# First five chunks of a retention and spatial-gating kernel evicted in two steps with ready tables, and the steps of its head newly ordered

## Chip, cores and metric

The kernel runs on one core of a Trainium2 chip. The metric is the device time of one execution in microseconds; of several executions the median counts.

## What is computed

Inputs are q, k, v of shape (4, 8, 768, 64), float32. First a linear attention with a decay per head (retention), then an MLP with a spatial gate:

```python
state = gamma * state + outer(k[t], v[t])
y[t] = scale * (q[t] @ state)
x = y as (4, 768, 512)
h = relu(x @ w_in);  u, v = h[..., :512], h[..., 512:]
v_n = (v - mean(v)) / sqrt(var(v) + 1e-6)
v_s = w_spatial @ v_n + b_spatial
out = (u * v_s) @ w_out
```

## The kernel before

The work is cut into 24 chunks of 128 positions, six for each of four batches. Within a chunk two heads share the 128 partitions, so that a chunk is four head pairs. A chunk of retention has these steps. `scale_values` (letter p) multiplies v by the inverse decay; a first digit chooses the engine, and `p202` to `p206` are eight ScalarE instructions each. `ret_scores` (q) makes the products of keys and queries, `ret_mask` (j) masks them on VectorE. `total_sum` (t) adds the outer products of k and v to a running sum in PSUM, for half a chunk at a time, and with a first digit 1 it issues the next chunk's scores between. `total_copy` (k) copies this sum to SBUF, two ScalarE copies for each half. `out_products` (y) makes the chunk's output in two halves. `out_evict` (E) takes it out of PSUM, multiplied by the decay of its position. `out_half` splits it into a high part (h, rounded to float32r) and a low part (l). From chunk 5 on the sum is rebuilt per chunk (S and x).

The weights arrive as int64 words that hold doubles. Each of twelve pieces goes through a (ScalarE), c0 to c4 (VectorE), H (ScalarE: rounded high part), R and Q (VectorE or GpSimd: low part). Three float32r products (high times high, high times low, low times high) stand for one exact product.

`v_products` (V) are 12 matmuls for each chunk: four pieces k, three products each. After these come r (relu), s, A, e, w, n, N (normalization), u and z (the other half of w_in), P (spatial products), g, i, f, d (gate), o (output), Z (store).

The order of everything is written out by hand in the string `STEPS` (lines 24 to 85), one word per step. Each engine runs its own steps strictly in that order, through `keep`, and so does the SyncE queue that issues the loads (G, J: groups of q, k, v; L: weights; K: spatial weights; B: bias). So a step that waits holds back all that stands behind it on the same engine. U is a matmul on zeros into a PSUM tile that nobody reads; ten of them run before the first data arrive, and eight more stand between the steps of the first chunks.

What the change touches lies mostly before the word u7 of `STEPS`, some 96 us into the span: batch 0 and the weights. The multiplication at the eviction (lines 475 to 482) is one instruction for each head pair, with two factors:

```python
nc.vector.scalar_tensor_tensor(
    xf[:, hp], t[hp % 2][:, hp // 2].rearrange("p i c -> p (i c)"),
    qg_t[:, c, hp : hp + 1], qd_t[:, hp], ALU.mult, ALU.mult)
```

`qd_t` (the decay within a chunk) is a table that the kernel makes itself: VectorE spreads 8 columns over a diagonal (`decay_rows`, line 828), one float32 matmul spreads the rows over the partitions (`decay_spread`), ScalarE copies the result (`decay_copy`, line 835).

Of the kernel before, what the change touches and what calls it, by code (L numbers as in the profile page):

```python
# [9 lines left out]
F32 = mybir.dt.float32  # L10
# [80 lines left out]
THIRD = (5, 6)  # L91
SPLIT = ((0, 1), (2, 3), (4, 7), (12, 13), (5, 6), (10, 8), (9, 11))
# [3 lines left out]
def tile_retention_gmlp(  # L96
# [8 lines left out]
    decay: bass.AP,  # L105
    out: bass.AP,
# [24 lines left out]

    mask_t = wpool.tile([P, C], F32, name="mask_t")
    ND = 3 * NC * NP
    consts_t = wpool.tile([P, ND + NP * P // C], F32, name="decay_t")
# [4 lines left out]

    LINE = 64 // 4  # L140
# [99 lines left out]
    def split_high(i):  # L240
        keep(nc.scalar.copy(doubles[i][0], halves[i][1]))
# [35 lines left out]
    def spatial_high(n, s):  # L277
        keep(nc.scalar.copy(parts_sp[n][0][:, s], wholes[n][s]))

    def spatial_low(n, s):  # L280
        high, low = parts_sp[n]
        keep(residue(nc.vector, low[:, s], wholes[n][s], high[:, s]))
# [526 lines left out]
    for r in ROWS:  # L809
        nc.gpsimd.memset(pick_t[r, r], 1.0)  # L810
# [120 lines left out]
```

## Time and profile before

| | us |
|---|---|
| median of 3 runs | 369.53 |
| lowest, highest | 369.22, 370.04 |
| the profiled execution, its own time | 370.09 |
| its span, first to last instruction | 368.1 |
| TensorE busy | 360.3 |
| VectorE busy | 238.0 |
| ScalarE busy | 156.1 |
| GpSimd busy | 114.5 |

The span is what the trace shows; 2.0 us of the execution's own time lie around it. Matmuls overlap, and their modelled ends make TensorE look busier than it is, so that a stretch with little useful work can still read 80% busy. The distance between the starts of two matmuls tells more than their durations.

### The profile page before, as it was taken

The numbers are of one execution on the slowest core, as the hardware profiler recorded it, in microseconds if no ns is written. First come the engines' busy times: TensorE is split into PE (matmuls) and PEld (weight loads), VectorE is DVE, ScalarE is ACT, GpSimd is POOL, SyncE is SP. The second block draws the span as 40 slices with busy tenths as digits, with TensorE's granted clock in tenths as the row PEclk, the third lists the DMA queues.
The fourth block names the chain that finished last, engine by engine and source line by source line (L and its number), as shares of the span: only waits on it lengthen the run. The fifth ranks groups of instructions, "written<-read, shape, count | busy, mean of one in ns | idle before, by whom it ended". The sixth has DMA issues, their size and how long they took to land.

```text
span 368.1 us, 10328 instructions
## 1 busy us (share of the span) xinstructions
PE 360.3 (98%) x4428; PEld 314.0 (85%) x4428; DVE 238.0 (65%) x533; ACT 156.1 (42%) x322; POOL 114.5 (31%) x121
## 2 busy tenths in 40 slices
PE   7899999999999999999999999999999999999996
PEld 3677885879888889998988889999998888999985
DVE  2997999698875767698585562368685452165631
ACT  3797784443423355632313246342232235432232
POOL 3612531371053324241425341133133322404011
PEclk9999999999999999999999999999999999999999
DMA  7974786002253530303333214123303002000022
GB/s 303 397 265 190 294 312 268 0 12 105 88 174 116 173 120 28 116 3 116 116 115 119 84 59 144 36 80 116 118 0 122 24 2 87 0 0 2 1 87 85
DMA packets 13005, 41.20 MB, mean 112 GB/s; under 512 B 1440, under 2 KB 1696, under 8 KB 12960
## 3 DMA queue, kind: packets, MB, share of 16 engines
q1 hardware_dynamic: 12816, 40.42, 29.6%
q8 instruction: 35, 0.57, 0.7%
q10 hardware_dynamic: 144, 0.13, 0.1%
q14 instruction: 10, 0.08, 0.1%
HBM read 34.25 MB, written 6.29 MB: 110 GB/s over the span
## 4 chain that ended last, share of the span: by engine, by line
PE 93%; DMA 2%; ACT 1%; SPq 1%; DVE 1%; issue 0%; POOL 0%; POOLq 0%
PE u L161 18%; PE v L161 18%; PE o L161 18%; PE y L161 10%; PE sp L161 8%; PE x L161 6%; PE z L161 5%; PE s L161 3%; PE w L161 3%; PE d L161 2%; DMA vk<-in_float_dram 2%; PE total L161 1%; SPq L164 1%; ACT third L345 1%; ACT third L378 0%
## 5 line engine op out<-in xcount | busy, mean ns | idle before, releaser
L161 PE MATMUL u<-xh,winu_w 128*128 128x384 f32 x256 | 68.3, 338 | 0.0
L161 PE MATMUL v<-winv_w,xh 128*128 128x512 f32 x192 | 60.6, 397 | 0.0
L161 PE MATMUL o<-wout_w,gh 128*128 128x512 f32 (+1 forms) x192 | 59.3, 390 | 0.0
L475 DVE SCALAR_TENSOR_TENSOR xf<-x,decay_t,qd_t 128x128 f32<-128x128 f32 x96 | 29.2, 343 | 31.3 <-PE x L161 25.2
L161 PEld LDWEIGHTS u<-xh,winu_w 128*128 128x128 f32 x256 | 46.5, 188 | 0.7
L161 PE MATMUL u<-xl,winu_w 128*128 128x384 f32 x128 | 42.8, 335 | 0.0
L161 PE MATMUL y<-sp,a 128*128 128x384 f32 x216 | 41.8, 336 | 0.0
L161 PEld LDWEIGHTS v<-winv_w,xh 128*128 128x128 f32 x192 | 35.2, 188 | 7.4
L161 PEld LDWEIGHTS o<-wout_w,gh 128*128 128x128 f32 x192 | 35.2, 188 | 6.8
L573 POOL TENSOR_TENSOR vn<-vn 128x384 f32<-128x384 f32 x24 | 24.8, 1032 | 49.7 <-DVE a L167 40.5
L589 ACT CAST a<-vn 128x384 fp32r<-128x384 f32 x42 | 21.0, 512 | 42.8 <-POOL vn L573 26.7
L161 PE MATMUL v<-winv_w,xl 128*128 128x512 f32 x96 | 37.6, 392 | 0.8 <-issue 0.8
L161 PEld LDWEIGHTS y<-sp,a 128*128 128x128 f32 x216 | 37.6, 188 | 0.4
L161 PE MATMUL o<-wout_w,gl 128*128 128x512 f32 (+1 forms) x96 | 37.2, 388 | 0.0
L167 DVE TENSOR_TENSOR a<-vn,a 128x384 fp32r<-128x384 f32 x42 | 23.7, 577 | 13.5 <-ACT a L589 13.2
L650 ACT ACTIVATE ur<-u 128x384 f32<-128x384 f32 x32 | 15.2, 488 | 36.1 <-PE u L161 31.0
L539 POOL TENSOR_TENSOR rs<-rs,mhalf 128x1 f32<-128x1 f32 x24 | 15.0, 631 | 49.3 <-DVE rs L535 46.4
L352 POOL TENSOR_TENSOR vk<-vk,decay_t 128x512 f32<-128x512 f32 x17 | 19.1, 1123 | 35.9 <-DMA vk<-in_float_dram 35.9
L526 DVE BATCH_NORM_STATS2 bst<-vr 128x6 f32<-128x512 f32 x24 | 16.4, 687 | 18.9 <-ACT vr L519 18.9
L161 PE MATMUL s<-qk 64*64 64x64 f32 x768 | 27.8, 220 | 0.0
L161 PEld LDWEIGHTS s<-qk 64*64 64x64 f32 x768 | 25.0, 135 | 2.5 <-issue 2.2
L428 DVE TENSOR_TENSOR ws<-d,ws 64x256 f32<-64x256 f32 x54 | 22.8, 422 | 6.4 <-PE d L161 4.9
(120 smaller groups left out, 670.8 us busy)
## 6 DMA issues: line engine op xcount, KB each, us to landing
qk<-in_float_dram SPq DMA_DIRECT2D x24, 512.0 KB, 4.7
vk<-in_float_dram SPq DMA_DIRECT2D x20, 512.0 KB, 4.9
raw<-in_int_dram SPq DMA_DIRECT2D x12, 512.0 KB, 6.3
out_dram<-ot SPq DMA_DIRECT2D x23, 256.0 KB, 2.0
wst<-in_float_dram SPq DMA_DIRECT2D x4, 576.0 KB, 7.1
third<-in_float_dram SPq DMA_DIRECT2D x3, 512.0 KB, 9.2
values<-in_float_dram SPq DMA_DIRECT2D x1, 552.0 KB, 4.3
bsp_t<-in_float_dram SPq DMA_DIRECT2D x1, 384.0 KB, 6.0
```

Of the source, the lines that this page charges most:

```text
L161: keep(nc.tensor.matmul(out, lhs, rhs, start=start, stop=stop, skip_group_check=shared))
L164: keep(nc.sync.dma_start(dst, src))
L167: return eng.tensor_tensor(out, whole, high.bitcast(F32), ALU.subtract)
L345: keep(nc.scalar.mul(v, v, f))
L352: keep(engine.tensor_tensor(values[g], values[g], vd, ALU.mult))
L428: keep(nc.vector.tensor_tensor(dst[ROWS[r]], u, states[g][ROWS[r], i], ALU.add))
L475: nc.vector.scalar_tensor_tensor(xf[:, hp], t[hp % 2][:, hp // 2].rearrange("p i c -> p (i c)"), qg_t[:, c, hp : hp + 1], qd_t[:, hp], ALU ...
L526: keep(nc.vector.bn_stats(st, norm[b, c][0]))
L539: keep(nc.gpsimd.tensor_tensor(rs, rs, mhalf, ALU.pow))
L573: nc.gpsimd.tensor_tensor(*{7: (a11, a11, a21, ALU.subtract), 5: (a21, a21, a22, ALU.add), 6: (a21, a22, a11, ALU.subtract), 3: (a21, a12, ...
L589: keep(nc.scalar.copy(t[:, 0], part_whole(b, p, m)))
L650: keep(nc.scalar.activation(u, pu[:, :HALF], AF.Relu))
```

## The change

Four parts. (1) Chunks 0 to 4, and 6, 12 and 18 (the first ones of the other batches), are evicted by two `tensor_tensor` on two head pairs each, with one factor, instead of four `scalar_tensor_tensor`. (2) Each of the first five chunks has its own ready table. The host sends decay rows cut into three bf16 parts, 30 rows with a selection matrix beside them (69 KB), loaded by a DMA that ScalarE issues (m20). For each table one bf16 matmul spreads them over the partitions (m0 to m4, 30 rows by 512 columns) and ScalarE copies the result (m10 to m14). The diagonal product on VectorE and its GpSimd memsets and selects go. (3) Many steps may choose their engine by a digit: some relus, rounded copies and residues go from ScalarE to VectorE or from VectorE to GpSimd or back. V can be issued in two parts, two products that need only the high weights (V1...) and the one that needs the low weights (V2...). (4) The words of `STEPS` up to u7 are newly ordered; after that only four E words go.

```diff
-    "G0 v p0 U10 q0 j0 L0 L2 a0 m2 t00 m0 k000 k001 t01 y00 U301 y01 c00 c01 c02 c03 a2 c20 c21 "
-    "c22 G1 k011 k010 H0 m1 E00 L1 U201 U101 U501 q1 p1 t10 k100 k101 a1 t11 U401 U701 G2 k111 "
-    "E02 c23 E01 k110 E03 h0 j1 y10 c04 c24 c10 y11 E10 E13 E12 E11 c11 c12 p202 t20 k201 k200 L3 "
-    "a3 H1 h1 R0 Q0 l0 q2 V00 G3 G4 t21 k211 k210 c13 c30 c31 j2 l101 c14 q3 y20 y21 G5 E20 E23 "
-    "E22 E21 j3 c32 R101 Q1 p203 t130 k301 k300 U601 V10 U801 H2 h2 l102 t131 j4 k310 k311 p204 "
-    "y30 y31 E30 E31 R102 Q102 c33 c34 V20 t140 L5 k401 k400 H3 E32 a5 E33 h3 c50 c51 c52 l103 "
-    "c53 c54 V01 V21 V11 V22 V12 t141 k411 k410 R3 Q3 V02 V03 V23 y40 p205 t50 y41 E40 E41 E42 "
-    "E43 L4 r0 r2 k501 s0 A0 a4 h4 k500 c40 c41 j5 G6 G7 q6 V13 V30 V31 V32 V33 H5 R5 y50 y51 s2 "
...
+    "U10 G0 q0 U301 p100 m20 m0 m10 m1 L0 j0 a0 c00 t00 k000 y00 m3 m13 U201 c01 c02 c03 k001 y01 "
+    "t01 G1 E00 E02 k011 c04 q1 k010 m11 v p1 j1 h0 L2 a2 m2 c20 l100 c21 L1 a1 c10 U101 U501 "
+    "U401 L3 t10 k100 k101 t11 c22 c23 c24 a3 y10 y11 E10 G2 k111 H0 q2 m12 U701 U601 k110 R100 "
+    "p202 t20 c30 k201 k200 U801 E12 m4 j2 Q0 G3 p203 V1000 V2000 G4 t21 k211 y20 y21 q3 h101 "
+    "l101 c11 c12 c13 c14 L5 k210 t130 H1 V1010 V2010 V1011 V1001 G5 k301 E20 E22 k300 j3 h2 y30 "
+    "t131 y31 R01 H2 c31 l102 V1020 m14 Q101 V2001 V2011 V1012 p204 V1002 R102 Q02 V2020 V1021 "
+    "V2021 V2002 L4 c32 k311 G6 E30 V1022 j4 E32 V2022 a5 k310 t140 L6 c33 H3 V1003 c34 a4 c40 "
+    "V2012 h3 G7 k400 k401 c41 c42 R103 Q3 y40 c50 t141 k411 k410 y41 E40 p205 E42 V1023 V1013 j5 "
+    "V2013 c51 c52 V2003 r100 h4 V2023 s0 t50 k501 c53 k500 q6 l03 y50 y51 E50 E52 E53 V1030 a6 "
+    "A0 e0 r2 l4 s2 E51 H5 R5 c54 A2 e2 w2 h5 c43 c44 L8 l105 w0 n0 V2030 V1031 V2031 V1032 V1040 "
...
+    "V2052 K0 u1 V1053 z1 Q04 a8 W1 a9 L10 c60 c61 c62 c63 c90 c91 w3 H6 n3 N3 V2053 R06 r105 s5 "
+    "a7 c92 A5 w4 n4 N4 c93 u4 e5 z4 w5 n5 N5 S6 x600 G8 c80 c70 c71 c72 c64 u0 c73 Q106 c81 c82 "
+    "B P1 g1 i1 f1 P2 c74 P0 c83 H8 c84 R8 H7 z0 d01 H9 R109 c94 Q09 g0 u2 z2 g2 W2 Q108 a10 c100 "
...
         t, xf = evicted[g]
         outs[g] = xf
+        if c == 0 or g < TABLES:
+            for n in (s // 2 for s in steps if s % 2 == 0):
+                both = t[n].rearrange("p h i c -> p h (i c)")
+                keep(nc.vector.tensor_tensor(xf[:, n::2], both, tables[c][:, n::2], ALU.mult))
+            return
...
+        three = ((xh, high), (xh, low), (xl, high))
+        for x, w in (three, three[::2], three[1:2])[part]:
+            n = begun[b, c] = begun.get((b, c), 0) + 1
+            mm(norm[b, c], x[:, k, cols], w, start=n == 1, stop=n == 3 * KT)
...
-    def decay_copy():
-        keep(nc.scalar.copy(qd_t.rearrange("p h c -> p (h c)"), spread.pop(0)))
+    def decay_load():
+        keep(nc.scalar.dma_start(sown_t, rows))
+
+    def decay_spread(c):
+        spread[c] = ps_m.tile([P, NP * P], F32, tag="m", name=f"spread{c}")
+        mm(spread[c], pick_t[:, c * P : c * P + P], rows_t, True, True)
+
+    def decay_copy(c):
...
+        keep(nc.scalar.copy(tables[c].rearrange("p h c -> p (h c)"), spread.pop(c)))
```

## Rows read from the trace of the kernel before

**Rows 1.** The page: its span, busy time of TensorE, granted clock in 40 slices.
```profile
span 368.1 us, 10328 instructions
...
PE 360.3 (98%) x4428; PEld 314.0 (85%) x4428; DVE 238.0 (65%) x533; ACT 156.1 (42%) x322; POOL 114.5 (31%) x121
...
PEclk9999999999999999999999999999999999999999
```

**Rows 2.** Windows: us, busy of the engines (instructions), clock, DMA share, GB/s.
```profile
10.00:15.00 5.00, 4.08 (x104) 2.96 (x100) 4.92 (x12) 3.04 (x7) 2.74 (x2) 1.00 1.03 416
...
50.00:60.00 10.00, 10.00 (x40) 7.06 (x39) 9.83 (x23) 6.97 (x12) 3.15 (x4) 1.00 1.02 408
```

**Rows 3.** Waits of TensorE: us in total, times, longest.
```profile
PE total L161 <- ACT ws L378: 0.9, 1, 0.9
PE v L161 <- issue: 0.8, 1, 0.8
```

**Rows 4.** Chain that ended last, from 21 to 43 us: start, us, what.
```profile
21.33 1.16 PE x L161 x64
...
30.85 0.75 issue
...
40.96 1.09 PE x L161 x64
```

**Rows 5.** DMA issues, one short window each (issued 3.73, 4.22, 4.75, 5.76 us).
```profile
raw<-in_int_dram SPq DMA_DIRECT2D x1, 512.0 KB, 8.9
...
qk<-in_float_dram SPq DMA_DIRECT2D x1, 512.0 KB, 10.8
...
third<-in_float_dram SPq DMA_DIRECT2D x1, 512.0 KB, 11.5
...
raw<-in_int_dram SPq DMA_DIRECT2D x1, 512.0 KB, 11.8
```

**Rows 6.** Timeline of ScalarE: start, us, line, operation, names, idle before.
```profile
16.38 2.02 ACT L345 ACTIVATE third<-third,decay_t 128x64 f32<-128x64 f32 x8
18.43 0.75 ACT L378 COPY third<-total 64x256 f32<-64x256 f32 x2
...
21.46 2.02 ACT L345 ACTIVATE vk<-vk,decay_t 128x64 f32<-128x64 f32 x8
...
32.86 0.75 ACT L378 COPY third<-total 64x256 f32<-64x256 f32 x2 [2.06 <-PE total L161]
```

**Rows 7.** Groups by shape, ScalarE and VectorE, 5 to 45 us: busy, mean ns.
```profile
L207 ACT ACTIVATE room<-raw 128x512 f32<-128x512 f32 x6 | 4.0, 675 | 2.0 <-DMA raw<-in_int_dram 1.9
...
L241 ACT CAST winv_w<-df 128x512 fp32r<-128x512 f32 x4 | 2.5, 618 | 0.0
...
L835 ACT COPY qd_t<-spread 128x512 f32<-128x512 f32 x1 | 0.6, 586 | 0.0
...
L475 DVE SCALAR_TENSOR_TENSOR xf<-x,decay_t,qd_t 128x128 f32<-128x128 f32 x24 | 6.9, 341 | 2.0 <-PE x L161 1.9
```

**Rows 8.** The page, its groups of instructions and its DMA issues.
```profile
L428 DVE TENSOR_TENSOR ws<-d,ws 64x256 f32<-64x256 f32 x54 | 22.8, 422 | 6.4 <-PE d L161 4.9
...
out_dram<-ot SPq DMA_DIRECT2D x23, 256.0 KB, 2.0
```

**Rows 9.** Timelines of VectorE and GpSimd where the two meet.
```profile
15.39 1.49 DVE L212 TENSOR_SCALAR room<-room 128x512 f32<-128x512 f32 x1
...
16.81 1.12 DVE L475 SCALAR_TENSOR_TENSOR xf<-x,decay_t,qd_t 128x128 f32<-128x128 f32 x4
...
15.01 1.59 POOL L249 TENSOR_TENSOR winv_w<-df,room 128x512 fp32r<-128x512 f32 x1 [0.73 <-DVE room L238]
...
16.56 1.46 POOL L167 TENSOR_TENSOR xl<-xf,xh 128x512 fp32r<-128x512 f32 x1
```

**Rows 10.** Chain that ended last, where TensorE never waits: start, us, what.
```profile
113.90 1.09 PE x L161 x64
...
126.64 6.12 PE v L161 x27
```

More of the change, by code (lines that the diff above doesn't have):

```diff
@@ L91 @@
 THIRD = (5, 6)
+SOWN = 7
+TABLE_ROOMS = (10, 11)
+TABLES = 5
+PARTS = 3 * 2 * TABLES
+SOWN_COLS = (TABLES * 128 + 512) // 2
 SPLIT = ((0, 1), (2, 3), (4, 7), (12, 13), (5, 6), (10, 8), (9, 11))
@@ L105, in tile_retention_gmlp @@
     decay: bass.AP,
+    rows: bass.AP,
     out: bass.AP,
@@ L130, in tile_retention_gmlp @@
     ps_o = ctx.enter_context(tc.tile_pool(name="ps_o", bufs=3, space=bass.MemoryType.PSUM))
+    LINE = 64 // 4
     mask_t = wpool.tile([P, C], F32, name="mask_t")
     ND = 3 * NC * NP
-    consts_t = wpool.tile([P, ND + NP * P // C], F32, name="decay_t")
+    consts_t = wpool.tile([P, -(-ND // LINE) * LINE], F32, name="decay_t")[:, :ND]
     decay_t = consts_t[:, :ND].rearrange("p (n t h) -> p n t h", t=3, h=NP)
@@ L170, in pick, with copied, positive @@
         return (nc.gpsimd, nc.vector, nc.scalar)[int(n)]
+    def copied(out, src, on_vector):
+        return (nc.vector.tensor_copy if on_vector else nc.scalar.copy)(out, src)
+    def positive(out, src, on_vector):
+        if on_vector:
+            return nc.vector.tensor_scalar(out, src, 0.0, None, ALU.max)
+        return nc.scalar.activation(out, src, AF.Relu)
     doubles = [
@@ L238, in split_low, with split_high @@
         keep(nc.vector.scalar_tensor_tensor(a, low, 2.0**-52, a, ALU.mult, ALU.mult))
-    def split_high(i):
-        keep(nc.scalar.copy(doubles[i][0], halves[i][1]))
+    def split_high(i, on_vector):
+        keep(copied(doubles[i][0], halves[i][1], on_vector))
     def split_rest(i, engine):
@@ L275, in spatial_sum, with spatial_high, spatial_low @@
         parts_sp[n] = [slot(SPLIT[n][i], F32R, f"sp{n}_{i}") for i in range(2)]
-    def spatial_high(n, s):
-        keep(nc.scalar.copy(parts_sp[n][0][:, s], wholes[n][s]))
-    def spatial_low(n, s):
+    def spatial_high(n, s, on_vector):
+        keep(copied(parts_sp[n][0][:, s], wholes[n][s], on_vector))
+    def spatial_low(n, s, engine):
         high, low = parts_sp[n]
-        keep(residue(nc.vector, low[:, s], wholes[n][s], high[:, s]))
+        keep(residue(engine, low[:, s], wholes[n][s], high[:, s]))
     queries = {}
@@ L318, in load_values @@
             t = slot(ROOM0, F32, "values0").rearrange("p s c -> p (s c)")
-            t = first[0] = t[:, : 4 * NP * C + ND + NP * P // C]
+            t = first[0] = t[:, : 4 * NP * C + ND]
             load(t, decay)
@@ L460, in tile_retention_gmlp @@
     evicted = {}
+    tables = {0: qd_t}
     def out_evict(g, steps=range(NP)):
@@ L483, in out_evict, with out_half @@
             )
-    def out_half(g, low, engine=None):
+    def out_half(g, low, engine=None, on_vector=False):
         b, c = divmod(g, NC)
@@ L491, in out_half @@
         else:
-            keep(nc.scalar.copy(xh[:, :, cols], outs[g]))
+            keep(copied(xh[:, :, cols], outs[g], on_vector))
     def split3(pairs, ps, start=True, stop=True):
@@ L503, in tile_retention_gmlp, with v_products, v_relu @@
     norm = {}
-    def v_products(b, c, ks=range(KT)):
+    begun = {}
+    def v_products(b, c, k, part=0):
         xh, xl = xhalf[b, c // TT]
         cols = slice((c % TT) * P, (c % TT) * P + P)
-        if not ks[0]:
+        if (b, c) not in begun:
             norm[b, c] = ps_m.tile([P, DM], F32, tag="m", name=f"v{b}_{c}")
-        split3(
-            [((xh[:, k, cols], xl[:, k, cols]), (winv_h[:, k], winv_l[:, k])) for k in ks],
-            norm[b, c],
-            start=not ks[0],
-            stop=ks[-1] == KT - 1,
-        )
-    def v_relu(b, c):
+        high, low = winv_h[:, k], winv_l[:, k]
+        three = ((xh, high), (xh, low), (xl, high))
+        for x, w in (three, three[::2], three[1:2])[part]:
+            n = begun[b, c] = begun.get((b, c), 0) + 1
+            mm(norm[b, c], x[:, k, cols], w, start=n == 1, stop=n == 3 * KT)
+    def v_relu(b, c, on_vector):
         v = mpool.tile([P, DM], F32, tag="v", bufs=3, name=f"vr{b}_{c}")
-        keep(nc.scalar.activation(v, norm[b, c], AF.Relu))
+        keep(positive(v, norm[b, c], on_vector))
         norm[b, c] = [v]
@@ L568, in corners, with part_sum @@
         return [vn[b][:, s, d] for d in cols for s in rows]
-    def part_sum(b, p, m):
+    def part_sum(b, p, m, engine):
         a11, a12, a21, a22 = corners(b, p)
         keep(
-            nc.gpsimd.tensor_tensor(
+            engine.tensor_tensor(
                 *{
@@ L585, in part_whole, with part_high, part_low @@
         return {1: a11, 2: a12, 4: a22, 7: a11}.get(m, a21)
-    def part_high(b, p, m):
+    def part_high(b, p, m, on_vector):
         t = pieces[p, m] = pair_room(F32R, f"a{b}_{p}_{m}")
-        keep(nc.scalar.copy(t[:, 0], part_whole(b, p, m)))
-    def part_low(b, p, m):
+        keep(copied(t[:, 0], part_whole(b, p, m), on_vector))
+    def part_low(b, p, m, engine):
         t = pieces[p, m]
-        keep(residue(nc.vector, t[:, 1], part_whole(b, p, m), t[:, 0]))
+        keep(residue(engine, t[:, 1], part_whole(b, p, m), t[:, 0]))
     held = {}
@@ L645, in mlp_u, with u_relu @@
         us[b, half, j] = pu
-    def u_relu(b, j, half):
+    def u_relu(b, j, half, on_vector):
         pu = us[b, half, j]
         u = mpool.tile([P, HALF], F32, tag="u", name=f"ur{b}_{j}_{half}", bufs=6)
-        keep(nc.scalar.activation(u, pu[:, :HALF], AF.Relu))
+        keep(positive(u, pu[:, :HALF], on_vector))
         us[b, half, j] = u
@@ L674, in gate_product @@
     def gate_product(b, j, half):
-        pp, u = gate[b, half, j], us[b, half, j]
+        pp = gate[b, half, j]
         t = mpool.tile([P, HALF], F32, tag="t", name=f"t{b}_{j}_{half}", bufs=3)
@@ L678, in gate_product, with gate_high @@
         keep(nc.vector.tensor_tensor(t, pp[:, :HALF], bsp_t[:, cols], ALU.add))
-        gate[b, half, j] = t, u
+        gate[b, half, j] = t
     def gate_times(b, j, half):
-        t, u = gate[b, half, j]
+        t, u = gate[b, half, j], us[b, half, j]
         keep(nc.vector.tensor_tensor(t, t, u, ALU.mult))
         gate[b, half, j] = t
-    def gate_high(b, j, half):
+    def gate_high(b, j, half, on_vector):
         t = gate[b, half, j]
         gh = mpool.tile([P, HALF], F32R, tag="gh", name=f"gh{b}_{j}_{half}")
-        keep(nc.scalar.copy(gh, t))
+        keep(copied(gh, t, on_vector))
         gate[b, half, j] = (t, gh)
@@ L767, in tile_retention_gmlp @@
         "E": lambda n: out_evict(n // 10, [n % 10]),
-        "h": lambda n: out_half(n, False),
+        "h": lambda n: out_half(n % 100, False, None, n // 100),
         "l": lambda n: out_half(n % 100, True, pick(n // 100)),
-        "V": lambda n: v_products(*divmod(n // 10, NC), [n % 10]),
-        "r": lambda n: v_relu(*divmod(n, NC)),
+        "V": lambda n: v_products(*divmod(n % 1000 // 10, NC), n % 10, n // 1000),
+        "r": lambda n: v_relu(*divmod(n % 100, NC), n // 100),
         "s": lambda n: v_stats(*divmod(n, NC)),
@@ L780, in tile_retention_gmlp @@
         "W": spatial_sum,
[L781 to L782 removed]
+        "X": lambda n: spatial_high(n // 10 % 10, n % 10, n // 100),
+        "Y": lambda n: spatial_low(n // 10 % 10, n % 10, pick(1 - n // 100)),
         "u": lambda n: mlp_u(n // 10, *units[n % 10]),
[L784 removed]
+        "z": lambda n: u_relu(n // 10 % 10, *units[n % 10], n // 100),
         "P": lambda n: spatial_products(0, *units[n]),
@@ L802, in tile_retention_gmlp @@
     wps = ps_m.tile([P, DM], F32, tag="m", name="wps")
-    sown_t = pair_room(F32, "sown").rearrange("p n s c -> p (n s c)")
-    pick_t, eye_t = sown_t[:, :P], sown_t[:, P : P + C]
-    rows_t = sown_t[:, P + C : P + C + NP * P]
     spread = {}
-    nc.gpsimd.memset(pick_t, 0.0)
-    for r in ROWS:
-        nc.gpsimd.memset(pick_t[r, r], 1.0)
+    sown_t = slot(SOWN, F32, "sown").rearrange("p s c -> p (s c)")[:PARTS, :SOWN_COLS]
+    pick_t = sown_t.bitcast(BF16)[:, : TABLES * P]
+    rows_t = sown_t.bitcast(BF16)[:, TABLES * P :]
     nc.gpsimd.memset(mask_t, 1.0)
@@ L815, in tile_retention_gmlp @@
         )
-    nc.gpsimd.memset(eye_t, 1.0)
-    for r in ROWS:
-        nc.gpsimd.affine_select(
-            eye_t[r], eye_t[r], [[1, C]], ALU.is_equal, 0.0, base=0, channel_multiplier=-1
-        )
-    def decay_rows():
-        n = NP * P // C
-        eye = eye_t.unsqueeze(2).broadcast_to([P, C, n])
-        own = first[0][:, 4 * NP * C + ND :].unsqueeze(1).broadcast_to([P, C, n])
-        rows = rows_t.rearrange("p (c n) -> p c n", n=n)
-        keep(nc.vector.tensor_tensor(rows, eye, own, ALU.mult))
-    def decay_spread():
-        spread[0] = ps_m.tile([P, NP * P], F32, tag="m", name="spread")
-        mm(spread[0], pick_t, rows_t, True, True)
-    def decay_copy():
-        keep(nc.scalar.copy(qd_t.rearrange("p h c -> p (h c)"), spread.pop(0)))
+    def decay_load():
[4 more added lines that the diff above has]
+    def decay_copy(c):
+        if c and c % 2:
+            t = slot(TABLE_ROOMS[c // 2], F32, f"tables{c}").rearrange("p s c -> p (s c)")
+            for n in range(2):
+                tables[c + n] = t[:, n * NP * P : n * NP * P + NP * P].rearrange(
+                    "p (h c) -> p h c", h=NP
+                )
+        keep(nc.scalar.copy(tables[c].rearrange("p h c -> p (h c)"), spread.pop(c)))
     rooms = []
@@ L884 @@
     vdecay = vdecay.transpose(1, 4, 2, 3, 0).reshape(P, NC, 2, NP)
-    qd = (grown[:, :P] / np.sqrt(D)).reshape(NP, 2, P).transpose(1, 0, 2).reshape(2, NP * P)
+    qd = (grown / np.sqrt(D)).reshape(NP, 2, NC, P).transpose(2, 1, 0, 3)
+    qd = qd.reshape(2 * NC, NP * P)[: 2 * TABLES].astype(np.float32)
+    parts = []
+    for _ in range(3):
+        high = (qd.view(np.uint32) & 0xFFFF0000).view(np.float32)
+        parts.append(high)
+        qd = qd - high
+    picks = np.tile(np.repeat(np.eye(2 * TABLES, dtype=np.float32), C, 1), (3, 1))
+    parts = np.concatenate([picks, np.concatenate(parts, 0)], 1)
+    parts = (parts.view(np.uint32) >> 16).astype(np.uint16).view(np.float32)
     qg = (gamma[:, None] ** (P * np.arange(NC))).reshape(NP, 2, 1, NC)
@@ L899 @@
     }
-    head = arrays["groups"][0, 1], arrays["decay"], qd.reshape(P, -1).astype(np.float32)
-    arrays["decay"] = np.concatenate(head, 1)
+    arrays["decay"] = np.concatenate([arrays["groups"][0, 1], arrays["decay"]], 1)
+    arrays["rows"] = parts
     nc = _bacc.Bacc("TRN2", target_bir_lowering=False, num_devices=1, dynamic_dma_scratch_size=1024)
```

16 lines of the change are left out of this document (6 added, 10 removed), and 101 rows, old and new, of the table STEPS.

## Prediction, made before any run of the changed kernel

> **What bounds the kernel now.** I read the page first. TensorE is busy for 360.3 of 368.1 us, and the granted clock is at full speed in all 40 slices [rows 1]. So the time is the sum of TensorE's work, plus what it waits at the start, plus a tail. A change that leaves the work alone can only change the waiting. The list of TensorE's waits seems to leave nothing: 0.9 us for the running sum's copies, 0.8 us under the name "issue" [rows 3]. This is misleading, because the modelled ends of overlapping matmuls cover short waits. In the stretch from 10 to 15 us TensorE reads 4.08 of 5.00 us busy, yet its 104 instructions are nearly all matmuls of 64 columns [rows 2]. Where nothing holds it, 64 of those start within 1.09 us [rows 10]; 104 are worth 1.8 us, and the rest is waiting. From 50 us on it is busy throughout [rows 2].
>
> So I priced the work by the distances between starts where TensorE never waits: 27 matmuls of V in 6.12 us, 0.227 us each, and 1.09 us for both output halves (y) of a chunk [rows 10]. The 596 matmuls of 64 columns (0.017 us each) and the 33 of V that start in the first 35 us are 10.1 + 7.5 = 17.6 us of work by these prices, so 17.4 us are not work; after 42 us nothing worth naming is lost. Some 5.4 us of it pass before the first chunk is there and scored. All that the change can win lies between 6 and 42 us, and after the word u7 both orders are the same.
>
> The chain of waits says what holds TensorE there. The operands of chunk 2 land at 4.75 + 11.5 = 16.3 us [rows 5]; ScalarE scales them in 2.02 us from 16.38 and copies the sum in 0.75 us from 18.43 [rows 6]; chunk 2's output starts at 21.33 and the next running sum, t130, after it, at 22.49 [rows 4]. VectorE has 4.92 of 5.00 us in the same stretch and the DMA engines are full [rows 2]: four resources are near their limit at once.
>
> **The change part by part.** *Evictions.* Four instructions of 0.341 us mean [rows 7], four in 1.12 us back to back [rows 9], become two with 256 columns. The nearest row is the addition out of PSUM with 256 columns, 0.422 us [rows 8]; it has 64 partitions and not 128, but the length goes by columns. Two take 0.68 to 0.84 us, so a chunk saves 0.3 to 0.45 us of VectorE, five chunks about 1.9 us. Chunks 6, 12 and 18 save as much where TensorE is never short: nothing there. The diagonal product goes too, but VectorE takes over chunk 0's scaling, of the same length. None of this is on the path by itself: in the new order the outputs that TensorE then needs wait for ScalarE. I count it as nothing, covered by VectorE having 0.2 to 1 us in hand at each use; without that cover it would be worth up to 1.9 us.
>
> *Tables.* Five bf16 matmuls instead of one in float32: they lie where TensorE waits anyway, so nothing. Five ScalarE copies of 0.586 us [rows 7] instead of one are 2.3 us more in ScalarE's queue; two rounded copies or relus moved to VectorE in this stretch give 1.2 back. The first three delay the copies k001 and v and with them chunk 1's scaling on GpSimd by some 0.5 us, which the later load absorbs; the fourth is hidden behind the third load, the fifth (m14, 0.5 us) stands in a full queue and is in the walk below. The table rows' own DMA is behind no row of this trace. Lower bound: landed 2.0 us after its issue near 2.3 us, as a store takes [rows 8]. Upper bound: behind all SyncE loads, 17.5 us [rows 5]. It is a seventh of the size of a load and does not stand in SyncE's order, so I take the lower end; up to some 7 us it costs nothing, since the first copy of the sum waits for the first weights anyway.
>
> *Loads, and the start of t130.* The new order issues L0, G1, L2, L1, L3 and only then G2. Chunk 2's keys and values move from eighth and ninth place to ninth and tenth. The tenth load lands at 5.76 + 11.8 = 17.5 us, where the ninth was at 16.3 [rows 5]. ScalarE then needs 2.02 for p202, 0.75 for two copies, 2.02 for p203, which now stands ahead of the next two copies, and 0.75 for these [rows 6]: 17.6 + 5.54 = 23.1 us for t130. Before it was 22.49. **Term 1: +0.6 us.** Equal work is behind both at this point.
>
> *From t130 to chunk 5's output.* Before, this ends at 40.96 + 1.09 = 42.05 [rows 4] and lasts 19.56 us, of which 12 matmuls of V for chunk 3 (12 x 0.227 = 2.72) are work that the new order does later: 16.84 us. The work common to both is 33 matmuls of V (7.5), six output halves (3.3), four sums with or without the scores of the next chunk (2.8), one without and one set of scores alone (1.1): 14.7 us. So the old order loses 2.1 us: 0.75 as "issue" [rows 4], some 0.4 to two matmuls on zeros, the rest around the sums. In the new order the V products are dealt out between the sums, and half of them can start before the low parts of the weights are there. I walked each engine's queue by hand with durations of the rows. TensorE then runs through from 23.1 to 37.3. ScalarE's queue in the same time, from p202 to the last copy k500, is 18.3 us of work by rows 6 and 7, and with what it waits for TensorE (as it does now, 2.06 us before one pair of copies [rows 6]) it ends near 37.7. So the second half of chunk 5's output waits some 0.5 us. 14.7 + 0.5 = 15.2. **Term 2: 15.2 - 16.8 = -1.6 us.**
>
> *The rest up to u7.* The set of matmuls is the same. VectorE's load there is about even (three relus and three residues more, seven residues of gate and spatial weights fewer). TensorE gets u4 ahead of the spatial products and so has 2.1 us more in hand while the last normalization is due. Against that stand GpSimd's new steps. A scalar instruction of VectorE that takes 0.43 us took 1.49 us at 15.39, ending just after GpSimd's residue of 15.01 to 16.60; the evictions at 16.81 ran four in 1.12 us beside GpSimd's next one [rows 9]. VectorE ran at 9.83 of 10 us from 50 to 60 [rows 2]. One such block there is 1.0 us, of which half is in hand; I take 0.2, between 0 and 1.0. **Term 3: +0.2 us.**
>
> The Trainium skill, page "SBUF — State Buffer", section "Who interferes with whom", states this as a rule: copies and scalar instructions of VectorE in the two-port mode, and those with two inputs in SBUF, take a port pair that GpSimd shares, and who comes second is fully blocked. By that rule each rounded copy given to VectorE and each residue given to GpSimd makes a new meeting, which speaks against part 3 of the change; term 3 would be +1.0 by it. The two rows at 15.39 and 16.81 agree with the rule [rows 9].
>
> **Sum:** +0.6 - 1.6 + 0.2 = -0.8 us. The profiled execution has a span of 368.1 and took 370.09, 0.56 above the median of 369.53. So the span becomes 367.3 and the median 368.7. A measurement of this kernel can tell 0.2%, 0.74 us, from no change: the forecast is just outside.
>
> **The rivals.** *A: the gain is given back at the spatial products.* P1 needs all six normalized chunks, and the next one needs the bank that g1 empties on VectorE; by my walk both are only 0.5 us ahead. With two blocks of 1.0 us as in rows 9, or with the "issue" gap of 0.75 us coming back elsewhere, the gain falls by 0.7 to 1.0: about 369.4. For it: VectorE's 9.83 of 10. Against: u4 in hand. *B: ScalarE's queue becomes the bound, slower than before.* From 17.6 to 37.7 us it has 18.3 us of work, now with p203 ahead of copies that TensorE waits for and with the table copy m14. If it loses more than some 1.0 us besides (a late weight piece before a4 or a5, an eviction before h3), every sum from t140 on waits, and the three or four waits of 0.5 to 0.7 us add 1.9: -0.8 + 1.9 = +1.1, 370.6. For it: term 1, and that ScalarE stands in strict order. Against: V products between the sums. *C: a larger gain.* Between the landings of the seventh and eighth loads lie 2.4 us (3.73 + 8.9 = 12.6 and 4.22 + 10.8 = 15.0), between the others some 1.3 [rows 5]. If that pause is not tied to a time, chunk 2's values land 1.1 us sooner; term 1 becomes -0.5, and VectorE's saved 1.9 us may free another 0.2: 367.4. *That the two steps are no shorter than the four* (two at 0.5 us and over) would cost VectorE under 0.2 us a chunk, within what it has in hand.
>
> **How the numbers follow.** Forecast 0.45, A 0.22, B 0.16, C 0.17. The forecast's own range is 368.1 to 369.2, for term 3's bounds and the wait in term 2; about three quarters of it lie over 0.2% faster. Faster: 0.34 + 0.17 = 0.51, with a little of A 0.52. Same: the rest of the forecast and most of A, 0.30. Slower: B and a trace of A, 0.18. The range reaches to C and B: 366.9 to 370.6.
>
> **What would show it.** Chunk 2's scaling should start near 17.6 us, t130 near 23.1, chunk 5's output should end near 38.3, the first float32 spatial product should start near 54, and u7 near 95.3 instead of 96.1. An eviction should read two instructions of about 0.42 us. Waits of TensorE for ScalarE's copies after 30 us would show B; long scalar instructions of VectorE beside GpSimd after 45 us with TensorE waiting for g1 or the last normalization would show A. I am wrong if TensorE's own work per step changes, if the table rows land after some 7 us, which would hold the first sum back behind m0, or if the clock falls in the head: in rows 1 it stands at full speed throughout, with TensorE as idle as it was there.

## The result, and the profile after

The changed kernel takes 371.96 us, the median of 20 runs (370.11 to 373.56), against 369.53 for the kernel before. The ratio is 1.006, 95% interval 1.0046 to 1.0074: slower by 2.4 us. The forecast was 368.7, faster, with a range to 370.6.

The profiled execution of the changed kernel took 371.79 us. Its page:

```profile
span 370.0 us, 10294 instructions
...
PE 360.8 (98%) x4428; PEld 314.9 (85%) x4431; DVE 236.4 (64%) x521; ACT 153.8 (42%) x318; POOL 116.3 (31%) x118
...
PEclk9999999999999999999999999999999999999999
```

Little is to be seen here: against [rows 1] no engine's busy time differs by more than 2.3 us (ScalarE 2.3 less, GpSimd 1.8 more), and the clock reads full speed in 40 slices. The windows of the head, in the columns of [rows 2], say more; the third line is the second window in the kernel before:

```profile
10.00:15.00 5.00, 3.39 (x89) 2.51 (x90) 3.83 (x8) 3.52 (x9) 1.04 (x1) 1.00 1.02 414
15.00:20.00 5.00, 3.92 (x113) 3.41 (x114) 4.83 (x12) 4.88 (x15) 1.21 (x1) 0.67 0.82 310
...
15.00:20.00 5.00, 4.98 (x145) 3.74 (x141) 4.63 (x10) 4.87 (x16) 3.01 (x2) 1.00 0.96 372
```

TensorE starts 89 matmuls between 10 and 15 us where it started 104 before, and from 15 to 20 us the granted clock is 0.67 of full speed. The trace's clock record says that it fell from 2.4 to 1.2 GHz at 16.71 us, after TensorE had stood still for 0.9 us at 13.3 and waited between the matmuls of the sums, and rose again at 20.12. A slice of the page is 9.25 us long and its digit 9 means 90% or more, so 1.8 us at half speed in one slice and 1.6 in the next cannot show there. What TensorE waited for (the counterpart of [rows 3]):

```profile
PE total L168 <- POOL vk L367: 0.9, 1, 0.9
PE total L168 <- ACT ws L393: 0.9, 1, 0.9
PE x L168 <- ACT ws L393: 0.6, 1, 0.6
```

The first and the third line are new. (The third, for the copies of chunk 0's sum, stands in `v_ahead` below as well, so it is not what decides.) The timeline of ScalarE shows where the first comes from:

```profile
7.82 0.58 ACT L850 COPY qd_t<-spread 128x512 f32<-128x512 f32 x1 [5.52 <-PE spread L168]
8.30 0.67 ACT L222 ACTIVATE room<-raw 128x512 f32<-128x512 f32 x1
8.99 0.37 ACT L393 COPY ws<-total 64x256 f32<-64x256 f32 x1
9.39 0.58 ACT L850 COPY tables<-spread 128x512 f32<-128x512 f32 x1
9.99 0.36 ACT L393 COPY ws<-total 64x256 f32<-64x256 f32 x1
11.49 0.74 ACT L393 COPY ws<-total 64x256 f32<-64x256 f32 x2 [1.14 <-PE total L168]
12.24 0.59 ACT L850 COPY tables<-spread 128x512 f32<-128x512 f32 x1
12.73 0.26 ACT L327 COPY decay_t<-values 128x72 f32<-128x72 f32 x1
...
18.26 2.02 ACT L360 ACTIVATE third<-third,decay_t 128x64 f32<-128x64 f32 x8
```

and GpSimd's only instruction between 2 and 16 us:

```profile
13.12 1.04 POOL L367 TENSOR_TENSOR vk<-vk,decay_t 128x512 f32<-128x512 f32 x1 [11.55 <-ACT decay_t L327]
```

The copy at 12.73 is the word v: 0.26 us that turn the decay factors into the form which the scalings read. Before, it was the second word and ran at 5.52 us, so that GpSimd waited for chunk 1's values alone:

```profile
5.52 0.26 ACT L312 COPY decay_t<-values 128x80 f32<-128x80 f32 x1 [3.24 <-DMA values<-in_float_dram]
...
11.53 1.34 POOL L352 TENSOR_TENSOR vk<-vk,decay_t 128x512 f32<-128x512 f32 x1 [4.84 <-DMA vk<-in_float_dram]
```

In the new order it stands behind the copies of chunk 0 and the table copy m11. Chunk 1's values had landed at 9.93, and GpSimd could scale them only at 13.12; the second running sum, t10, starts at 14.22 instead of 12.92. t130's first product on the running sum starts at 24.36 instead of 22.33 (the second line is the kernel before):

```profile
24.36 0.27 PE L168 MATMUL total<-vk 64*64 64x64 f32 x1
...
22.33 0.25 PE L161 MATMUL total<-vk 64*64 64x64 f32 x2
```

From there the chain of waits (counterpart of [rows 4]) goes as forecast; chunk 5's output ends at 39.64, where 38.3 was forecast with t130 1.3 us sooner:

```profile
38.60 1.04 PE x L168 x62
```

and the evictions are as short as forecast, 0.420 us each:

```profile
L492 DVE TENSOR_TENSOR xf<-x,tables 128x256 f32<-128x256 f32 x8 | 3.2, 420 | 1.4 <-PE x L168 1.3
```

At u7 the changed kernel is 0.6 us behind, at the last matmul 0.7; the span is 1.9 us longer. So more than 1 us is lost after the last matmul. The DMA view of the last microseconds (queue and kind: packets, MB, share; then the issue, KB, us to landing), after:

```profile
q14 instruction: 1, 0.01, 0.4%
...
out_dram<-ot_last ACTq DMA_DIRECT2D x1, 128.0 KB, 3.3
```

and of the kernel before, in which no instruction packet falls between this issue and its landing:

```profile
out_dram<-ot_last ACTq DMA_DIRECT2D x1, 128.0 KB, 2.2
```

The last store takes 3.27 us instead of 2.15. By the single packets of the trace, 8 KB of instructions are under way from 367.63 to 367.94 us; the store's last data packet ends at 367.63, its last completion word goes out only at 367.93, and the landing is noted at 368.97. In the old order the last completion word follows the data at once.

### The profile page after: what moved, and what is told of

The parts are those of the page before. It is cut to its first block, busy times and chain, and to the rows that moved or that the text cites. A ratio compares the mean times of both kernels' runs of the same rounds, so it can differ in the third digit from the quotient of the medians.

```text
span 370.0 us, 10294 instructions
## 1 busy us (share of the span) xinstructions
PE 360.8 (98%) x4428; PEld 314.9 (85%) x4431; DVE 236.4 (64%) x521; ACT 153.8 (42%) x318; POOL 116.3 (31%) x118
## 4 chain that ended last, share of the span: by engine, by line
PE 97%; ACT 1%; POOL 0%; issue 0%; DVE 0%; POOLq 0%
PE u L168 18%; PE v L168 18%; PE o L168 18%; PE y L168 10%; PE sp L168 8%; PE x L168 7%; PE z L168 5%; PE s L168 4%; PE w L168 3%; PE d L168 2%; PE wps L763 2%; PE total L168 1%; ACT ws L393 1%; PE o_last L168 0%; ACT tables L850 0%; POOL vk L367 0%
## 5 line engine op out<-in xcount | busy, mean ns | idle before, releaser
L168 PE MATMUL v<-winv_w,xh 128*128 128x512 f32 x192 | 61.4, 396 | 0.0
L496 DVE SCALAR_TENSOR_TENSOR xf<-x,decay_t,qd_t 128x128 f32<-128x128 f32 x64 | 19.7, 345 | 21.4 <-PE x L168 15.4
L367 POOL TENSOR_TENSOR vk<-vk,decay_t 128x512 f32<-128x512 f32 x17 | 19.1, 1124 | 38.3 <-DMA vk<-in_float_dram 25.6
L561 POOL TENSOR_TENSOR rs<-rs,mhalf 128x1 f32<-128x1 f32 x24 | 15.2, 635 | 47.5 <-DVE rs L557 47.5
L168 PE MATMUL s<-qk 64*64 64x64 f32 x768 | 28.6, 225 | 0.0
L168 PEld LDWEIGHTS s<-qk 64*64 64x64 f32 x768 | 25.9, 140 | 2.4 <-issue 1.2
L548 DVE BATCH_NORM_STATS2 bst<-vr 128x6 f32<-128x512 f32 x24 | 16.4, 688 | 18.0 <-ACT vr L185 17.9
```

What stands on the lines that cost most here:

```text
L168: keep(nc.tensor.matmul(out, lhs, rhs, start=start, stop=stop, skip_group_check=shared))
L367: keep(engine.tensor_tensor(values[g], values[g], vd, ALU.mult))
L496: nc.vector.scalar_tensor_tensor(xf[:, hp], t[hp % 2][:, hp // 2].rearrange("p i c -> p (i c)"), qg_t[:, c, hp : hp + 1], qd_t[:, hp], ALU ...
L548: keep(nc.vector.bn_stats(st, norm[b, c][0]))
L561: keep(nc.gpsimd.tensor_tensor(rs, rs, mhalf, ALU.pow))
```

## The experiments

Fourteen kernels, each timed in turn with the kernel before. Times are medians.

**1. The load of the table rows: `rows_on_sync`.**

```diff
-        keep(nc.scalar.dma_start(sown_t, rows))
+        keep(nc.sync.dma_start(sown_t, rows))
```

> The changed kernel with the load of the table rows issued by SyncE, third in its order, instead of ScalarE. Theory 'last store': in the changed kernel the very last store, which ScalarE issues, took 3.27 us from issue to landing, in the kernel before 2.15 us, because ScalarE's queue was used for a load before; then this kernel's last store takes about 2.15 us again and the time falls by 1.1 us, to about 370.8. Rival 'chance': the last store varies from run to run whatever was loaded; then the time stays at 371.9 and the store's landing is no shorter in the median. Rival 'head': the loads behind it land 0.2 us later, up to +0.3 us.

Measured 371.54 us, ratio 1.0064 (1.0043 to 1.0085). No difference, and the last store still takes 3.28 us; the rows land at 4.99 us in the changed kernel and hold nothing.

**2. `before_small_load`**: the kernel before, with an unread 69 KB load that ScalarE issues at the start.

> The kernel before with one added load of 69 KB that ScalarE issues at the start and that nobody reads. Theory 'last store': the last store takes about 3.3 us instead of 2.15, and the time rises by 1.1 us to about 370.6. Rival 'chance': the tail is as before, the time 369.5 to 369.8 (the added bytes are 0.2 us of the load queue).

Measured 369.45, ratio 1.0 (0.9988 to 1.0013), last store 2.2 us. A ScalarE load at the start does not make the last store long. This trace gave something else: it is a second execution of the old order, and at the place where the profile of before has "issue" [rows 4] it has nothing:

```profile
30.25 0.39 PE L161 MATMUL v<-winv_w,xl 128*128 128x512 f32 x1
30.47 0.62 PE L161 MATMUL v<-winv_w,xh 128*128 128x512 f32 x2
30.93 0.39 PE L161 MATMUL v<-winv_w,xl 128*128 128x512 f32 x1
```

**3. `zeros_in_gaps`**: fourteen more matmuls on zeros where TensorE waits.

```diff
-k001 y01 ... U501 U401 L3 ... k101 t11 ... U601 k110
+k001 U4 y01 ... U501 U401 U5 L3 ... k101 U3 t11 ... U601 U2 k110
```

> The changed kernel with 14 more matmuls on zeros where TensorE waits between 9 and 20 us (4 ahead of y01, 5 ahead of t10, 3 ahead of t11, 2 ahead of t20). Theory 'clock': the granted clock fell to half from 16.7 to 20.1 us in the changed kernel because TensorE had been idle too much between 9 and 16 us; with the gaps filled it stays at full speed from its first rise to the end, q2 takes 0.7 us instead of 1.4, t20 starts up to 1 us sooner, and the time falls by 0.6 to 1.0 us, to about 371.1. Rival 'queue': ScalarE's order alone sets the head, the clock hides in its waits; then the clock stays up but the time stays within 0.3 us of 371.9. Rival 'cost': the added matmuls themselves delay the sums, up to +0.5 us.

Measured 371.64, ratio 1.0058 (1.004 to 1.0075). The clock no longer falls, as the same window shows:

```profile
15.00:20.00 5.00, 4.90 (x136) 3.29 (x134) 4.91 (x11) 4.87 (x15) 1.39 (x1) 1.00 0.94 367
```

t130's sum starts at 23.56 instead of 24.36 in this trace, but the median is only 0.3 us lower, less than the intervals can tell. The trace is still 0.9 us ahead of the changed kernel at u7 and loses 0.8 of it later, 0.4 at 190 us under the name "issue". So what the fall costs by itself is not settled here; experiment 7 asks again.

**4. `copies_behind`**: v first, the table copies behind the copies of the sum.

```diff
-m20 m0 m10 m1 L0 ... y00 m3 m13 U201 ... k001 y01 ... m11 v p1 ... k111 H0 q2 m12 U701 U601 k110
+m20 v m0 m1 L0 ... y00 U201 ... k001 m10 y01 ... m11 p1 ... k111 k110 H0 q2 m12 m3 m13 U701 U601
```

> The changed kernel with the table copies moved behind the copies of the running sum in ScalarE's order: the copy of the decay constants (v) first, m10 behind k001, m11 behind k010 as before, m12 and m13 behind both copies of chunk 2's sum and H0; their matmuls moved with them. Theory 'queue': m10, m13 and m11 stood ahead of a0, k001 and v, and made chunk 1's scaling start at 13.12 us instead of about 11, and its copies at 14.95 instead of about 13.5; with them behind, the copies k100 start by 13.8, chunk 2's scaling at 17.3 when its values land, t130 by 23.3 instead of 24.57, and the time falls by 1.0 to 1.3 us, to about 370.8. Rival 'loads': chunk 2's landing at 17.3 us and what follows set t130; then t130 comes at most 0.7 us sooner and the time falls by no more than 0.7. Rival 'clock': if TensorE is idle as long as before between 9 and 16 us, the clock falls again and t20 starts as late as 20.1 us.

Measured 369.89, ratio 1.0013 (0.9997 to 1.0028): 2.1 of the 2.4 us are gone. Its last store took 2.2 us, so two causes went at once. (Its trace has one VectorE instruction more, 579 records against 578, and the instruction packet of the next experiment leaves at 361.26 us, ahead of the last store.) The next runs part them.

**5. The long last store: `three_more`, `before_47`, `v_bare`.** VectorE's stream has 582 instructions in the changed kernel, 599 in the one before (the traces hold 578 and 595 of them, 17 fewer either way). Three unread fills move every later packet of this stream:

```diff
+    for _ in range(3):
+        nc.vector.memset(idle_t, 0.0)
```

> The changed kernel with three unread 128x4 fills on VectorE at the start, nothing else. Theory F (a late instruction fetch): in the changed kernel, and in its two variants that end as late, an 8 KB packet of the instruction queue leaves at 367.6 us, in the middle of the last store, and that store needs 3.27 us from issue to landing instead of 2.15 as before; VectorE has 582 instructions there against 599 before, and the fetches seem to come each 128 instructions, so three more instructions move this one some microseconds ahead of the last store. F expects the last store at 2.2 us again and the median 1.1 us lower, 370.9 (ratio 1.003 to 1.004). Rival (the long store has to do with the ScalarE queue or with the later end, not with the fetch): store at 3.3 us, median 371.5 to 372.

Measured 371.05, ratio 1.0047 (1.003 to 1.0064): 0.9 us below the changed kernel. (Six of the 12 runs lie at 370.3 to 370.7 us and six at 371.4 to 372.6, with the median between, so prices taken from it can be off by some tenths.) The packet now leaves at 364.08, before the last store's issue at 367.66, and the store is short:

```profile
out_dram<-ot_last ACTq DMA_DIRECT2D x1, 128.0 KB, 2.2
```

> The kernel before with 47 unread 128x4 fills on VectorE at the start, where it waits for the first loads; 599 + 47 = 646 puts the end of its instruction stream at the same place past a multiple of 64 as the 582 of the changed kernel. Theory F: the last store takes 3.3 us instead of 2.2, median 369.5 + 1.1 = 370.6 (ratio 1.003). Rival: the store stays at 2.2 and the median at 369.5, or the fills delay the first zero matmuls and cost under 0.2 us.

Measured 370.05, ratio 1.0009 (0.9994 to 1.0023), store 2.2 us: a miss, and no test. No packet fell into the store. VectorE's packets leave near 64 + 128 n instructions in these traces (in the changed kernel behind 63, 185, 306, 446 and 575 records), and I had taken any multiple of 64. In all 13 traces of the new order the last one leaves behind 574 to 576 records, whether this is at 352 or at 369 us. `v_bare` repeats the test with `v_ahead` (below) without its fills, 582 instructions again:

> v_ahead without its three fills, so that only the word v is moved against the changed kernel; VectorE then has 582 instructions, as many as the changed kernel. Theory F (the late fetch): an 8 KB packet of the instruction queue leaves during the last store again, the store takes 3.3 us instead of the 2.2 of v_ahead, and the median is 0.9 to 1.1 us above v_ahead's 369.64: 370.5 to 370.8. Rival: store at 2.2, median within 0.2 us of v_ahead. (before_47 did not test this: the packets of VectorE's stream come at 64 + 128 n instructions, and 640 is none of these.)

Measured 370.75, ratio 1.0037 (1.0022 to 1.0051), 1.1 us above `v_ahead`, and in its trace:

```profile
q14 instruction: 1, 0.01, 0.4%
...
out_dram<-ot_last ACTq DMA_DIRECT2D x1, 128.0 KB, 3.3
```

So the late packet is shown in both directions, on two pairs of kernels that differ by three fills: 0.9 and 1.1 us by the medians (0.5 and 1.3 by the ratios).

**6. The word v alone: `v_ahead`**, with the three fills.

```diff
-p100 m20 m0 m10 m1 ... k010 m11 v p1
+p100 m20 v m0 m10 m1 ... k010 m11 p1
```

> The changed kernel with the ScalarE step v (the copy of the decay factors that the scaling of chunk 1 waits for) ahead of the first table copy instead of behind the second copy pair, and the three fills of three_more. Theory Q (ScalarE's queue order): v moves from 12.7 to 6.0 us, the scaling p1 from 13.1 to about 10.0, and the second sum t10 from 14.2 to about 12.7, since k010 ends at 12.2; t130 then starts 0.6 to 1.2 us sooner than in three_more, half of what putting all copies behind gave, median 0.5 to 1.0 us below three_more. Rival (the table copies m10 and m13 ahead of the sum's copies are the whole of it): t10 hardly moves, median within 0.3 us of three_more.

Measured 369.64, ratio 1.0003 (0.9987 to 1.0019): 1.4 us below `three_more`. ScalarE and GpSimd now have

```profile
5.85 0.25 ACT L327 COPY decay_t<-values 128x72 f32<-128x72 f32 x1 [3.56 <-DMA values<-in_float_dram]
```

```profile
9.93 1.04 POOL L367 TENSOR_TENSOR vk<-vk,decay_t 128x512 f32<-128x512 f32 x1 [8.35 <-DMA vk<-in_float_dram]
```

and t10 starts at 12.59, t130's sum at 23.07. The clock stays up in this profile. Without fills the same word is worth 1.2 us (371.96 to 370.75); by the ratios the two are 1.6 and 0.8. All the table copies that `copies_behind` moved besides brought nothing more.

**7. The clock again, without the late packet: `zeros_three_more`.**

> zeros_in_gaps with the three fills: against three_more only the 14 zero matmuls that keep TensorE busy where it waits. They hold the clock (in zeros_in_gaps it stood at full speed from 5.8 us on). Theory K (the fall of the clock costs by itself what TensorE then does more slowly): t20 and t130 start 1 us sooner and the median is 0.8 to 1.0 us below three_more's 371.05: 370.1. Rival (the clock fell because TensorE waited, and the waits stay): median within 0.4 us of three_more.

Measured 370.91, ratio 1.0043 (1.0024 to 1.0062), 0.1 us below `three_more` (8 and 12 runs). By the medians the rival holds. The traces give the clock more: t130's sum starts at 23.67 against 24.33 in `three_more`, and t20, which `p202` lets start, at 18.90 against 20.08. This trace then stands 0.7 us at "issue" near 25 us, which `three_more` does not. In the changed kernel itself the three fastest of 20 executions (370.1 to 370.6 us) have a mean clock of 0.996 or more, which leaves no room for a fall of 3.4 us (half speed for so long takes 0.0046 off the mean); three others without it took 372.1 to 372.3. So what the fall costs by itself stays open, between nothing and some 0.8 us. It came with the waiting for v: in the profile of `v_ahead` it is gone.

**8. The evictions alone: `v_four_steps`.**

```diff
-        if c == 0 or g < TABLES:
+        if c == 0:
...
+        if g < TABLES:
+            steps = (steps[0], steps[0] + 1)
```

> v_ahead with the evictions of chunks 1 to 4 in four scalar_tensor_tensor again (the tables are still made and copied, and not read). This is what the two-step eviction is worth where nothing else is wrong. The prediction counted it at nothing, and at 1.9 us at most: 369.6 to 369.9 by the first, since each takes 0.34 to 0.4 us more of VectorE where VectorE has some tenths in hand; rival: VectorE is the bound between t130 and chunk 5's output, and four evictions cost 1.0 to 1.5 us, 370.6 to 371.1.

Measured 369.90, ratio 1.0006 (0.999 to 1.0022), 0.3 above `v_ahead` and within the noise of both. Halving the eviction's instructions is worth nothing that 12 runs can tell.

**9. The load order: `third_early`, `v_and_third`, `third_free`, `third_first`.** All put G2 ahead of L3, so that chunk 2's values land at 15.8 to 16.4 us in the traces, where `copies_behind` and `v_ahead` have 17.0 and 17.5. The first starts from `copies_behind`, the others from `v_ahead`; what else each moves stands in its expectation.

> The kernel with the table copies behind (copies_behind), with G2 ahead of L3 in SyncE's order, so that chunk 2's values land near 15.9 us instead of 17.0; m12 and m13 right behind k101, a3 behind k200, p203 behind k210, so that p202 stands first when the values land; and the three fills. Theory Q: p202 starts near 16.1 instead of 17.85, t130 near 21.5 instead of 23.4, and the time falls 1 to 2 us below copies_behind: 368.0 to 368.9, below the kernel before. Rival (the weights that now land later, or GpSimd and VectorE, take the place of it): t130 comes sooner but the end of chunk 5's output does not, time 369.5 to 370.5.

Measured 370.52, ratio 1.0032 (1.001 to 1.0054). A miss. In the profiled execution L1 landed late, and the copies of the sum stood behind a1:

```profile
14.09 0.66 ACT L222 ACTIVATE room<-raw 128x512 f32<-128x512 f32 x1 [1.70 <-DMA raw<-in_int_dram]
```

This execution took 373.15 us and is one of two far above the other ten (369.45 to 371.14). What holds those above the forecast no trace shows.

> v_ahead with G2 ahead of L3 in SyncE's order, a1 behind k101 (so that a late L1 holds no copy of the sum back, as it did for 2.4 us in third_early), k110 right behind k111, a3 behind k200 and p203 behind k210. Theory Q: chunk 2's values land near 16.2 us and p202 starts there instead of at 17.54; t130 starts near 22 instead of 23.1, and the time falls 0.8 to 1.2 us below v_ahead: 368.4 to 368.9, a ratio to the kernel before of about 0.998. Rival (the third weights, 1.2 us later, or VectorE's queue take the gain back before chunk 5's output): 369.5 to 370.

Measured 370.56, ratio 1.003 (1.0018 to 1.0042). p202 starts at 16.76, but c30, ahead of the mask j2 on VectorE, waits for the third weights, and chunk 2's output waits for j2. VectorE's timeline, then TensorE's waits:

```profile
20.14 0.43 DVE L227 TENSOR_SCALAR room<-room 128x512 f32<-128x512 f32 x1 [2.04 <-ACT room L222]
```

```profile
PE x L168 <- DVE third L413: 0.9, 1, 0.9
```

```diff
-p202 t20 k201 k200 a3 c30 U801 E12 m4 j2 Q0 ... h101 l101 c11
+p202 t20 k201 k200 a3 U801 E12 m4 j2 Q0 ... h101 l101 c30 c11
```

> v_and_third with the VectorE step c30 moved from ahead of the mask j2 to behind l101. In v_and_third c30 waited 2.0 us for a3 (now later, since L3 lands later), and j2 and chunk 2's output behind it; TensorE waited 0.9 us for j2. Load theory (chunk 2's place in the load order costs the new order what term 1 said, some 0.6 us or more): with j2 free, chunk 2's output starts near 20.8, t130 near 22.2 instead of 23.1 in v_ahead, and the median is 0.5 to 1.0 us below v_ahead's 369.64: 368.7 to 369.1. Rival (VectorE or the third weights' chain, 1.2 us later, take it back before chunk 5's output): 369.5 to 370.3.

Measured 369.42, ratio 0.9992 (0.998 to 1.0004): 1.1 us below `v_and_third` for one word, 0.2 below `v_ahead`. In the traces t130's sum starts at 21.64 against 23.07, and about 1.1 us of that lead stay at the spatial products; the medians show less of it.

> third_free with t21, k211, k210 and p203 ahead of the first products V1000 and V2000 and ahead of a3, so that nothing but the sum's own chain stands on ScalarE between p202 and t130. Load theory: p203 starts near 20.2, t130 near 21.5, median 0.2 to 0.5 us below third_free: 368.3 to 368.8, faster than the kernel before. Rival as for third_free, with a3 later still: c30 and the low parts of the third weights come too late for their V products, 369.5 to 370.5.

Measured 372.13, ratio 1.0065 (1.0051 to 1.008). A miss: with a3 behind p203 the third weights come too late for their products, and the wait only changes its name (the profiled execution, 370.96 us, is the fastest of the six, so the trace does not show all that the median has):

```profile
PE v L168 <- ACT winv_w L180: 1.3, 1, 1.3
```

No version is faster than the kernel before by more than its interval; `third_free` equals it.

## Why the prediction was wrong

**Term 1 was mis-sized: +0.6 was forecast, +2.0 came** (24.36 against 22.33; two other traces of the old order have 22.58 and 23.27). The step that failed is the sentence on the tables, "The first three delay the copies k001 and v and with them chunk 1's scaling on GpSimd by some 0.5 us, which the later load absorbs". I counted what the added copies take, 0.59 us each, and not where v now stood: it had moved past the whole of chunk 0 on ScalarE, from 5.5 to 12.7 us. GpSimd's scaling came 3.2 us after its data, not 0.5. The second half fails too: the load did not absorb it. Chunk 2's values landed at 17.30 as forecast, but p202, forecast near 17.6, started at 18.26 behind k111, H0, m12 and k110, and t20 at 20.11, behind the scores q2, which ran at half clock. The single word costs 1.2 to 1.4 us by the medians (experiment 6), with what the clock lost by it, and t130 comes 1.3 us sooner in the traces of `v_ahead` and `v_bare`: about the whole excess of term 1. With v ahead t130 starts at 23.07 and chunk 5's output ends at 38.32, where 23.1 and 38.3 were forecast.

**Term 2 was right in the new order and wrong in the old.** From t130 to the end of chunk 5's output 15.2 us were forecast; 39.64 - 24.36 gives 15.3. But the 16.8 that it was held against (17.0 when counted, as here, from t130's first product: 42.05 - 22.33 - 2.72) had a stall of that one execution in it: "So the old order loses 2.1 us: 0.75 as 'issue' [rows 4]". Two other traces of the old order do not have it there; with the same count `before_small_load` needs 41.26 - 22.58 - 2.72 = 16.0, and `before_47` 15.9:

```profile
22.58 0.25 PE L161 MATMUL total<-vk 64*64 64x64 f32 x2
...
40.96 0.30 PE L161 MATMUL x<-qk,third 64*64 64x64 f32 x8
```

So the gain was 0.6 to 0.7 us, not 1.6. The prediction had said that its execution lay 0.56 us above the median, and did not ask which of its rows made it so.

**Term 3, +0.2, was right**: +0.3 measured up to u7 in this trace, +0.7 in that of `v_ahead`, both within the bounds of 0 and 1.0. 2.0 - 1.7 (17.0 to 15.3) + 0.3 makes the 0.6 us by which u7 is late against the profiled execution.

**A term was missing.** The sum ended at u7, with the words "after the word u7 both orders are the same". The instructions are, but not their place in VectorE's stream: 17 fewer put an instruction packet into the last store, 0.9 to 1.1 us.

By the medians: v 1.2 to 1.4, the packet 0.9 to 1.1, and with both away the new order stands 0.2 us from the old (`v_ahead`, no difference by its interval). Together they make 2.3 of the 2.4.

**The smaller steps.** Evictions at 0.42 us, no gain on the path: right on both counts. The table rows' load: landed at 5.0 us, nearer the lower bound (4.3) than the upper (17.5), though 4.1 us after its issue and not 2.0, and on nobody's path. The clock: I had listed its fall as what would make me wrong, and it fell for 3.4 us; held up, it returns 0.3 and 0.1 us by the medians and up to 0.8 in the traces, and this lies within what v costs. Rival B named ScalarE's strict order as the danger, and placed it from 17.6 us on; it decided at 9 to 13 us. Rival A's mechanism shows in one execution. In the profile of `three_more` a weight piece was late, and VectorE and GpSimd met:

```profile
37.09 1.49 DVE L232 TENSOR_SCALAR room<-room 128x512 int32<-128x512 int32 x1
38.62 1.81 DVE L240 SCALAR_TENSOR_TENSOR df<-raw,room 128x512 int32<-128x512 int32 x1
```

```profile
37.02 1.28 POOL L174 TENSOR_TENSOR xl<-xf,xh 128x512 fp32r<-128x512 f32 x1
38.61 1.28 POOL L174 TENSOR_TENSOR xl<-xf,xh 128x512 fp32r<-128x512 f32 x1 [0.31 <-ACT xh L180]
```

The same two instructions take 0.58 and 0.69 us in the profile of the changed kernel, 0.9 and 1.1 us less. The rule that the prediction took from the Trainium skill, page "SBUF — State Buffer", section "Who interferes with whom", fits both, a scalar instruction and one with two inputs in SBUF: each starts just after GpSimd's (0.07 and 0.01 us) and ends 0.3 and 0.5 us after it. That is less than the 0.58 and 0.69 us that they take otherwise, so this trace does not show that they stood still for the whole of GpSimd's. How often an execution has such a meeting was not tried.

## What to carry to other kernels

When a step is moved in a strict queue, look for the shortest instructions that change place, not only for those that are added: here 0.26 us of copy moved past eight others cost five times its length, because another engine's data had been waiting for it. Before a stall is counted as something that a change removes, see whether a second execution has it, and whether the profiled one is the slow one. And an instruction count is itself a change: after it, compare the last store's time to landing and the instruction packets near the end.

## What the runs showed of the hardware

An 8 KB instruction packet that a VectorE stream of 582 instructions calls for near its end can fall between the last data packet of a store and its completion word, and makes the landing 1.1 us later (3.27 against 2.15 to 2.20 us; four profiles with the packet there, twelve without). The packet itself lasts 0.31 us; why the landing moves by more was not tried. Of the store's 16 completion words 15 go out as usual, and only the last one waits for the packet's end.

The pause in the landings belongs to no load. In the kernel before it lies between the seventh and eighth [rows 5]; in the changed one it lies between two others, issued at 4.83 and 5.20 and landed 2.4 us apart where most land 1.2 apart:

```profile
raw<-in_int_dram SPq DMA_DIRECT2D x1, 512.0 KB, 8.8
...
qk<-in_float_dram SPq DMA_DIRECT2D x1, 512.0 KB, 10.9
```

In `third_early` it was L1 that came after it, 2.9 us behind its forerunner. In every profile it lies somewhere from 11 to 16.2 us, so an order that leaves no time in hand behind one load is an order that some executions break.

The transfers themselves do not pause: the DMA engines move 414 GB/s from 10 to 15 us. What comes late is, in most profiles, the last of a load's 16 completion words alone: in `third_early` 15 of L1's have gone out at 12.23 us, the last at 14.07. In all 16 profiles a 16 KB instruction packet, 0.88 to 0.98 us long, leaves between 11.8 and 13.7 us, and the first or second load to land after that is the late one. So the pause looks like the late store on a larger scale; as no run moved this packet, its part is argued and not shown.

The stall of TensorE called "issue" wanders too: 30.85 us before, 25 us in `zeros_three_more` (0.7 us), 190 us in `zeros_in_gaps` (0.4 us), nowhere in `before_small_load`. What causes it stays open.
